# The beginning of an attention and two expert layers: another order for the first row of maxima and for unit 1's loads and halves

## The chip, the cores and the metric

The kernel runs on one core of a Trainium2 chip. The metric is the device time of one execution in microseconds (us); a core has the engines PE (matrix multiply), DVE (vector), ACT (activation functions), POOL (general purpose) and SP (which here only issues transfers). Each engine executes its own instructions strictly in the order in which the program lists them; ACT, POOL and SP also issue transfers (DMA) between the main memory and the core.

## The reference, cut to what matters

Attention with a decay bias over 4 batches of 8 heads, 576 positions and 64 columns, then a layer of 8 experts that are chosen token by token, then a layer with a convolution gate. Only the attention's start is touched:

```
scores = scale * q @ k.T                       # 576 x 576 per head
cum    = cumsum(max(s, 0))                     # decay, one number per position
scores = where(causal, -1e9, scores + min(-(cum_i - cum_j), 0))
attn   = exp(scores - max(scores)); attn /= sum(attn) + 1e-9
out    = attn @ v
x      = expert layer(out);  y = gated layer(x)
```

## The kernel before

**Units and steps.** The attention works in 8 units of 4 heads (two units to a batch). A unit has 14 steps; a step computes one 128x512 tile of scores on PE (`scores`, L481 with a mask L484), one step later ACT takes the exponentials (`weights`, L520, or the pair L525 and L526), two steps later DVE subtracts to get the low half (`rest`, L537), four steps later PE multiplies by v (`values`, L553). Tiles of scores are in three buffers `z`, so the scores of a step can only be written when the exps and the subtraction of three steps before are done.

**Halves.** Each f32 number of q and k is held as two f16 halves. For a unit: load q and k (`load`, L165), scale to the high half on ACT (`split_hi`, L258), subtract to get the low half on DVE or on POOL (`split_lo`, L264 or L266 and L267), turn both by transposing transfers that SP issues (`turn`, L276), copy one part on DVE (`copy`, L284). In unit 0 PE does the turning (`turned`, L297; evacuated by ACT at L300 and by DVE at L302). The last 64 positions of all heads ("tails") go the same way: `load_tail` L193, `tail_hi` L288, `tail_lo` L292, `turn_tail`, `copy_tail` L326, rows of the decay by `extra_tail` L322.

**Maxima.** Before a unit's scores can be used, a row of maxima must stand in its k tile: `stage_a` computes scores once without the low halves in pieces (PE L381 into two buffers `za`), DVE takes the maximum of each piece (L384, L412), PE turns them (`max_turn`, L449), ACT copies them (`max_out`, L454), and a small transfer of two issues puts them in place (`max_row`, L461; the tail's is L464). The scores of the unit (L481) read that row. For unit 0 this is done in halves: pieces 0 to 5 for heads 0 and 1 (`pa`, then `mt0a`, `mo0a`, `mr0a`), pieces 6 to 11 for heads 2 and 3 (`pb`, `pc`, `pd`, then `mtb`, `mob`, `mrb`), pieces 12 to 14 for the tails (`pt`, then `mtt`, `mot`, `mrt`). Unit 0's scores begin with heads 0 and 1 (seven steps, 0 to 6); step 7 is the first that needs the second half's row. For unit 0 ACT issues these transfers, for the others SP.

**What sets the order.** A table `PAR` of numbers. `start` gives each task of the beginning a time: negative ones run in that order ahead of step 0, others in the step of their whole part, ahead of that step's scores on PE. For units 1 to 7 the numbers are steps counted from the unit's first step (14 times its number): `load` and `loadq`, `at` (split k, split q, the two transposes, the extra rows), `cp` (the copies), `sv` (halves of v), `pa` and `pn` (first step and spread of the maxima's pieces), `mx` (turning the maxima). Because engines run in order, the number decides what an instruction waits behind on each engine.

Of the kernel before, what the change touches and what calls it, by code (L numbers as in the profile page):

```python
# [42 lines left out]
class Keep:  # L43
# [6 lines left out]
PAR = {'u1': {'sv': -6, 'pa': -7, 'pn': 5, 'mx': -3},  # L50
 'u2': {'at': (-24, -23, -21, -20.9, -20), 'cp': (-16, -15), 'lv': -11, 'sv': -2, 'pa': -14, 'pn': 8, 'mx': -6},
 'u3': {'load': -37, 'loadq': 1, 'at': (-33, -30, -28, -27, -26.9), 'cp': (-21, -20), 'sv': -1, 'pa': -20, 'pn': 14, 'mx': -6},
 'u': {'load': -51,
# [22 lines left out]
           'thk': -29,  # L76
           'hk1': -28,
           'hq1': -27,
           'wm': -26,
           'pa': -25,  # L80
           'mt0a': -24,
           'mo0a': -23,
           'mr0a': -22,
           'thq': -21,
           'lk1': -20,
           'tlk': -19,
           'tlq': -18,
           'lq1': -17,
           'xt': -16,
           'lk2': -15,  # L90
           'lq2': -14,
           'T1k': -13,
           'T1q': -12,
           'x1': -11,
           'ttk': 0.6,
           'ttq': 1.0,
           'pb': 1.1,
           'ct': 2.0,
           'pt': 2.1,
           'sv0': 2.4,  # L100
           'c2': 2.5,
           'mtt': 3.0,
           'mot': 3.1,
           'mrt': 3.2,
           'pc': 3.3,
           'pd': 4.0,
           'mtb': 5.0,
           'mob': 5.1,
           'mrb': 5.2,
           'z': 6.0,  # L110
# [9 lines left out]
def attention(tc, ctx, q, k, v, s, xd, rt, hook):  # L120
# [7 lines left out]
    nc = tc.nc  # L128
# [131 lines left out]
    def split_lo(u, n):  # L260
        i = AT[n]
        a, h = U[u, n].rearrange("p h c (t d) -> p (h c t) d", t=2), U[u, "h"][:, i]
        if u < 1 or (u, n) == (1, "k"):
            V.scalar_tensor_tensor(h[:, :, i], in0=a, scalar=scale[n], in1=h[:, :, 1 - i], op0=ALU.mult, op1=ALU.subtract)  # L264
        else:
            G.tensor_scalar(a, a, scale[n], 0.0, op0=ALU.mult, op1=ALU.add)  # L266
            G.tensor_tensor(h[:, :, i], a, h[:, :, 1 - i], op=ALU.subtract)  # L267
# [188 lines left out]
    def max_row(u, hs=slice(0, 4), tails=True):  # L456
        n, Q = 0, nc.sync if u else nc.scalar
        if hs:
            n = 4 * (hs.stop - hs.start)
            for e in range(2):  # L460
                Q.dma_start(U[u, 1][70:71, e, 1, 256 * hs.start:256 * hs.stop].rearrange("o (x c) -> o x c", c=128), U[u, "mr", key(hs)][n // 2 * e:n // 2 * e + n // 2])  # L461
        if tails:
            c = 256 * (u % 2)
            Q.dma_start(T1[70:71, u // 2, 1, c:c + 256].rearrange("o (r c) -> o r c", r=2), U[u, "mr", key(hs)][n:n + 2])  # L464
# [185 lines left out]
    copy(0, "q")  # L650
    for n in ("k", "q"):
        load(1, n)
    load_tail("q")
    todo, pieces, copies = {}, {}, {5: [(1, "k")], 6: [(1, "q")]}

    def plan(t, f):
        todo.setdefault(math.floor(t), []).append((t, len(todo), f))
# [13 lines left out]
    def second_a(r):  # L671
# [11 lines left out]
        mtb=lambda: max_turn(0, second, False), mob=lambda: max_out(0, second, False), mrb=lambda: max_row(0, second, False),  # L683
        xt=extra_tail, ct=copy_tail, lk2=lambda: load(2, "k"), lq2=lambda: load(2, "q"),
        T1k=lambda: [turn(1, e, slice(0, 1)) for e in range(2)], T1q=lambda: [turn(1, e, slice(1, 2)) for e in range(2)], x1=lambda: extra(1),
# [13 lines left out]
    for u in range(1, NU):  # L699
        t0 = u * PER  # L700
        c = PAR.get(f"u{u}", {}) if u < 4 else PAR.get("u", {})
        if u > 1:
            if u > 2:
                plan(t0 + c["load"], lambda u=u: load(u, "k"))
                plan(t0 + c["load"] + c["loadq"], lambda u=u: load(u, "q"))
# [872 lines left out]
```

## Time and profile before

| | us |
|---|---|
| time, median of 3 runs (lowest to highest) | 710.66 (709.4 to 717.71) |
| time of the profiled execution | 709.87 |
| its span in the profile | 708.2 |
| PE busy in the span | 644.5 (91%) |
| DVE busy | 451.3 (64%) |
| ACT busy | 390.4 (55%) |
| POOL busy | 253.1 (36%) |

An engine's busy time says how much of the span it worked; it does not say what the others waited for. The views below do: a timeline lists an engine's instructions in order with the wait ahead of them, and the table of windows gives the busy time, the granted PE clock and the transfers of a stretch.

### The profile page before, as it was taken

What the parts mean: (1) busy time and instruction counts of PE and PEld (TensorE: products, weight loads), DVE (VectorE), ACT (ScalarE), POOL (GpSimd) and SP (SyncE); (2) the same over time, 40 slices, a digit from 0 to 9 for tenths busy, and PEclk for the clock granted to TensorE, in tenths of its full rate; (3) what the DMA queues carried; (4) which work ended last, traced back from release to release, by engine and by line L of the source; (5) the groups of instructions that cost most, each with busy time, mean ns of one, the idle gap of its engine ahead of it and who ended that gap; (6) DMA issues with size and microseconds to landing.
All of it is one profiled execution on the core that took longest, in us unless ns stands there. A gap on an engine that the chain in (4) does not pass through costs nothing. (4 is left out here: it accounts for less than half of the span.)

```text
span 708.2 us, 15490 instructions
## 1 busy us (share of the span) xinstructions
PE 644.5 (91%) x5177; PEld 403.8 (57%) x5177; DVE 451.3 (64%) x858; ACT 390.4 (55%) x660; POOL 253.1 (36%) x358
## 2 busy tenths in 40 slices
PE   5478999899999656999999999999889999999997
PEld 2346778688888533444444444444367766665443
DVE  7565788978876699563886867763039975546000
ACT  5451867778688656552845564532049964645111
POOL 7635976646332049932254453433100000000000
PEclk9765799989999869999999999999999999999999
DMA  5964686755547436899999998944195000000111
GB/s 144 185 145 73 113 162 128 175 113 97 159 135 264 128 100 198 241 304 293 258 277 266 289 234 245 220 129 82 50 169 101 1 16 19 28 31 30 45 46 59
DMA packets 168828, 101.82 MB, mean 144 GB/s; under 512 B 119712, under 2 KB 147016, under 8 KB 168732
## 3 DMA queue, kind: packets, MB, share of 16 engines
q1 hardware_dynamic: 164712, 88.65, 51.7%
q0 software_dynamic: 3984, 11.99, 5.6%
q8 instruction: 47, 0.77, 0.5%
q14 instruction: 49, 0.40, 0.2%
q10 hardware_dynamic: 36, 0.00, 0.0%
HBM read 62.18 MB, written 15.31 MB: 109 GB/s over the span
## 5 line engine op out<-in xcount | busy, mean ns | idle before, releaser
L1188 PE MATMUL hp<-r,xt 128*128 x504 | 113.9, 383 | 6.6 <-ACT xt L1219 6.6
L1188 PE MATMUL yp<-r,ht 128*128 x504 | 112.2, 379 | 1.7 <-PEq L1295 1.1
L1386 PE MATMUL hp<-yt,wi 128*128 128x288 f16 x768 | 95.6, 286 | 2.6 <-DMA yt<-yd 2.6
L1434 PE MATMUL o<-wo,g 128*128 128x512 f16 x432 | 94.5, 379 | 0.0
L1386 PEld LDWEIGHTS <-wi 128*128 128x128 f16 x768 | 75.1, 98 | 23.5 <-DMA yt<-yd 2.8
L1188 PEld LDWEIGHTS <-xt 128*128 128x128 f16 x504 | 49.7, 99 | 67.1 <-ACT xt L1219 7.7
L1188 PEld LDWEIGHTS <-ht 128*128 128x128 f16 x504 | 48.5, 98 | 57.4 <-issue 1.8
L1144 DVE SCALAR_TENSOR_TENSOR r<-st,r 128x512 f32 (+3 forms) x80 | 70.8, 952 | 6.7 <-ACT r L1133 5.0
L1434 PEld LDWEIGHTS <-g 128*128 128x128 f16 x432 | 42.3, 98 | 49.5
L384 DVE TENSOR_REDUCE mx<-za 128x1 f32<-128x384 f32 (+4 forms) x97 | 57.4, 603 | 18.7 <-PE za L381 18.2
L1133 ACT ACTIVATE r<-st 128x512 f32 (+3 forms) x84 | 57.1, 763 | 22.1 <-SPq L1181 12.9
L525 ACT ACTIVATE phi<-z,lnes 128x512 f16<-128x512 f32 (+1 forms) x80 | 50.6, 633 | 33.0 <-PE z L484 31.5
L1249 POOL DMA_INDIRECT yd<-ys,idx x21 | 23.9, 1136 | 122.6 <-DVEq L1172 77.7
L481 PE MATMUL z<-k 71*128 71x256 f16 (+2 forms) x320 | 54.8, 298 | 12.1 <-DMA k<-mr 8.7
L537 DVE TENSOR_TENSOR plo<-z,phi 128x512 f16<-128x512 f32 (+1 forms) x80 | 48.2, 603 | 11.0 <-ACT z L526 10.5
L1403 DVE SCALAR_TENSOR_TENSOR c<-hb,cw,c 128x576 f32<-128x576 f32 x32 | 26.1, 816 | 35.5 <-ACT c L1397 35.5
L526 ACT ACTIVATE z<-z,lnes 128x512 f32<-128x512 f32 (+1 forms) x80 | 48.5, 607 | 0.0
L553 PE MATMUL o<-v,p 128*128 128x65 f32 x256 | 47.1, 297 | 0.0
L1437 ACT ACTIVATE s<-o 128x512 f32<-128x512 f32 x18 | 10.7, 597 | 63.2 <-PE o L1434 63.2
L1247 ACT ACTIVATE ys<-yp,pp 128x512 f16<-128x512 f32 x21 | 14.3, 683 | 53.6 <-PE yp L1188 35.7
L553 PE MATMUL o<-vv,phi 128*128 128x65 f16 (+1 forms) x512 | 43.2, 206 | 0.0
L553 PEld LDWEIGHTS <-phi 128*128 128x128 f16 x544 | 42.8, 111 | 0.0
(285 smaller groups left out, 1201.5 us busy)
## 6 DMA issues: line engine op xcount, KB each, us to landing
st<-in_moe_w_dram SPq DMA_DIRECT2D x8, 2048.0 KB
st<-in_moe_w_dram SPq DMA_DIRECT2D x24, 512.0 KB
out_dram<-s SPq DMA_DIRECT2D x18, 256.0 KB
st<-in_k_dram SPq DMA_DIRECT2D x16, 256.0 KB
st<-in_q_dram SPq DMA_DIRECT2D x16, 256.0 KB
xd<-xh SPq DMA_DIRECT2D x16, 256.0 KB
k<-in_moe_w_dram SPq DMA_DIRECT2D x8, 512.0 KB
s<-in_moe_w_in_dram SPq DMA_DIRECT2D x16, 256.0 KB
```

What stands on the lines that cost most here:

```text
L384: return lambda: V.tensor_reduce(out, z.rearrange("p (e c) -> p e c", e=m), axis=AX.X, op=ALU.max)
L481: PE.matmul(out, lhsT=ks[i], rhs=qs[i], start=first and not i, stop=False, skip_group_check=True)
L525: A.activation(hi[:, 0:n], z[:, 0:n], AF.Exp, bias=lnes, scale=1.0 / SC)
L526: A.activation(p[:, 0:n], z[:, 0:n], AF.Exp, bias=lnes, scale=1.0 / SC)
L537: (V if md == "a" else G).tensor_tensor(lo[:, 0:n], p[:, 0:n], hi[:, 0:n], op=ALU.subtract)
L553: PE.matmul(out, lhsT=w, rhs=x, start=first, stop=last, skip_group_check=True)
L1133: i = self.nc.scalar.activation(hi, src, AF.Copy, scale=self.scale[w])
L1144: i = nc.vector.scalar_tensor_tensor(lo, in0=src, scalar=sc, in1=hi, op0=ALU.mult, op1=ALU.subtract)
L1188: i = self.nc.tensor.matmul(out, lhsT=lhsT, rhs=self.rings[w][:, c, k, bass.ds(s, 1), f], **kw)
L1386: PE.matmul(st[x][:, n, 0:HN], lhsT=wi[:, c, k, m], rhs=t[:, n, a + k], start=k + a + c == 0, stop=k == 3 and a == 4)
L1403: V.scalar_tensor_tensor(c, in0=h[:, 1:S + 1], scalar=cw[:, m, 1:2], in1=c, op0=ALU.mult, op1=ALU.add)
L1434: PE.matmul(o, lhsT=g[:, a, k, 128 * i:128 * i + 128], rhs=wo[:, c, k], start=j == 0, stop=j == 23)
```

## The change

In the beginning's table the tasks are put in another order, and four lines follow from it.

- The first half's row of maxima (`mr0a`) is issued by SP, and not by ACT. On SP it stands between unit 1's load of k and its load of q (`ldq1` is a new task; ahead of it the tails of q are loaded, which came behind unit 1's loads).
- ACT copies the first maxima (`mo0a`) straight after the tail's high half of k; unit 1's high halves (`hk1`, `hq1`) stood ahead of it. `hk1` now follows the tail's high half of q, `hq1` the first exp.
- Unit 1's low half of q is made by DVE (was POOL) in step 2, and its transposes, its extra rows and the loads of unit 2 are issued in step 2 (were ahead of step 0).
- The pieces `pc` and `pd` come at 2.2 and 3.3 (were 3.3 and 4.0), the second row of maxima at 4.4 to 4.6 (was 5.0 to 5.2), the halves of v for unit 0 (`sv0`) at 5.4 (was 2.4).
- Units 2 and 3 have some numbers a step or two later; no load of units 3 and 4 is issued ahead of step 7.

The rows of the table `start` that the text speaks of, and the rest of the diff:

```
- 'u2': {'at': (-24, -23, -21, -20.9, -20), 'cp': (-16, -15), 'lv': -11, 'sv': -2, 'pa': -14, 'pn': 8, 'mx': -6},
+ 'u2': {'at': (-22, -21, -19, -18.9, -18), 'cp': (-14, -13), 'lv': -11, 'sv': -2, 'pa': -12, 'pn': 7, 'mx': -6},
...
-           'sv0': 2.4,
...
+           'sv0': 5.4,
...
-        if u < 1 or (u, n) == (1, "k"):
+        if u < 2:
...
-        n, Q = 0, nc.sync if u else nc.scalar
+        n, Q = 0, nc.sync if u or hs == first else nc.scalar
...
-    for n in ("k", "q"):
-        load(1, n)
     load_tail("q")
+    load(1, "k")
...
-                plan(t0 + c["load"], lambda u=u: load(u, "k"))
+                plan(max(t0 + c["load"], 7), lambda u=u: load(u, "k"))
```

The changed program's lines are one higher (L165 is L166 there). SP, ahead of and in step 0, before: the 12 small rows of the decay (L318), unit 1's k and q (L165, two transfers each), the tails of q (L193), the tails' decay rows (L322), unit 2's k and q, the four transposes of unit 1 (L276).

```order
L318 DMA k_138<-cp 1x4x256 x12
L165 DMA st_112<-in_k_dram 128x4x128 x2
L165 DMA st_112<-in_q_dram 128x4x128 x2
L193 DMA k_143<-in_q_dram 32x8x128 x4
L322 DMA t_141<-ext 3x4x512 x2
L165 DMA st_111<-in_k_dram 128x4x128 x2
L165 DMA st_112<-in_q_dram 128x4x128 x2
L276 DMA_TRANSPOSE k_391<-st_111 128x16x64 x4
L280 DMA k_139<-ex 3x2x1024 x2
L165 DMA st_112<-in_k_dram 128x4x128 x2
L165 DMA st_111<-in_k_dram 128x4x128 x2
```

The same place of SP after the change:

```order
L319 DMA k_138<-cp 1x4x256 x12
L194 DMA k_143<-in_q_dram 32x8x128 x4
L166 DMA st_112<-in_k_dram 128x4x128 x2
L462 DMA k_138<-mr 1x4x128 x2
L166 DMA st_112<-in_q_dram 128x4x128 x2
L323 DMA t_141<-ext 3x4x512 x2
L277 DMA_TRANSPOSE k_384<-st_111 128x16x64 x4
L281 DMA k_139<-ex 3x2x1024 x2
L166 DMA st_111<-in_k_dram 128x4x128 x2
L166 DMA st_112<-in_q_dram 128x4x128 x2
```

The first row of maxima (L462) is new on SP, in front of unit 1's q; unit 2's loads moved from ahead of unit 1's transposes to behind its extra rows.

ACT, from the tail's high half of k (L288) on, before; L258 is unit 1's high halves, L454 and L461 the first maxima, L300 the tails' evacuation, L520 the exp of step 0, L341 the halves of v:

```order
L288 ACTIVATE k_144<-k_143 128x16x64
L258 ACTIVATE st_111<-st_112 128x16x64 x2
L454 ACTIVATE mr<-mt 8x128
L461 DMA k_138<-mr 1x4x128 x2
L288 ACTIVATE k_144<-k_143 128x16x64
L300 ACTIVATE t_142<-o 128x4x128 x4
L520 ACTIVATE p_473<-z,lnes 128x512
L341 ACTIVATE vv<-nv 128x16x64
L341 ACTIVATE vvt<-nvt 128x2x64
L525 ACTIVATE phi<-z,lnes 128x512
L526 ACTIVATE z<-z,lnes 128x512
L454 ACTIVATE mr<-mt 2x128
```

After, the same stretch, and what follows it:

```order
L289 ACTIVATE k_144<-k_143 128x16x64
L455 ACTIVATE mr<-mt 8x128
L289 ACTIVATE k_144<-k_143 128x16x64
L259 ACTIVATE st_111<-st_112 128x16x64
L301 ACTIVATE t_142<-o 128x4x128 x4
L521 ACTIVATE p_462<-z,lnes 128x512
L259 ACTIVATE st_111<-st_112 128x16x64
L526 ACTIVATE phi<-z,lnes 128x512
L527 ACTIVATE z<-z,lnes 128x512
L455 ACTIVATE mr<-mt 2x128
L465 DMA t_141<-mr 1x2x128
L521 ACTIVATE p_539<-z,lnes 128x512
```

```order
L521 ACTIVATE p_539<-z,lnes 128x512
L455 ACTIVATE mr<-mt 8x128
L462 DMA k_138<-mr 1x4x128 x2
L526 ACTIVATE phi<-z,lnes 128x512
L527 ACTIVATE z<-z,lnes 128x512
L342 ACTIVATE vv<-nv 128x16x64
L342 ACTIVATE vvt<-nvt 128x2x64
L526 ACTIVATE phi<-z,lnes 128x512
L527 ACTIVATE z<-z,lnes 128x512
```

The copy of the first maxima (now L455) moved up past three instructions and its transfer left ACT; one of unit 1's two high halves (L259) now stands between the exps of steps 0 and 1, and the halves of v (L342) between those of steps 3 and 4.

DVE, from unit 1's low half of k (L264) to the first maximum of the tails (L384, 128x2, behind the copies L326), before and after:

```order
L264 SCALAR_TENSOR_TENSOR st_111<-st_112,st_111 128x16x64
L292 SCALAR_TENSOR_TENSOR k_144<-k_143,k_144 128x16x64 x2
L302 CAST t_142<-z 128x4x128 x4
L384 TENSOR_REDUCE mx<-za 128x2 x2
L326 COPY t_141<-t_142 64x4x512 x2
L384 TENSOR_REDUCE mx<-za 128x2
L412 ISA za,mx<-za,zero,mx 128x512
```

```order
L293 SCALAR_TENSOR_TENSOR k_144<-k_143,k_144 128x16x64 x2
L265 SCALAR_TENSOR_TENSOR st_111<-st_112,st_111 128x16x64
L303 CAST t_142<-z 128x4x128 x4
L385 TENSOR_REDUCE mx<-za 128x2 x2
L327 COPY t_141<-t_142 64x4x512 x2
L265 SCALAR_TENSOR_TENSOR st_111<-st_112,st_111 128x16x64
L385 TENSOR_REDUCE mx<-za 128x2
L413 ISA za,mx<-za,zero,mx 128x512
```

Unit 1's low half of k (L265 after) moved behind the two low halves of the tails (L293), and the low half of q came to DVE, between the tails' copies (L327) and the tails' maxima.

## Rows read from the trace of the kernel before

**Rows 1.** The page's first line.

```profile
span 708.2 us, 15490 instructions
```

**Rows 2.** Waits of PE over the span: engine, line, releaser: us, times, longest.

```profile
PE z L481 <- DMA k<-mr: 8.7, 2, 5.7
```

**Rows 3.** Timeline of PE: start, length, engine, line, operation [idle before <-releaser].

```profile
18.88 0.39 PE L449 MATMUL mt<-ident,mx 128*8 128x128 f32 x2 [0.78 <-DVE mx L384]
...
28.20 1.04 PE L481 MATMUL z<-k 71*128 71x512 f16 x2 [5.74 <-DMA k<-mr]
...
32.77 0.87 PE L481 MATMUL z<-k 71*128 71x128 f16 x6
...
36.33 0.69 PE L481 MATMUL z<-k 71*128 71x512 f16 x2
...
39.84 1.06 PE L481 MATMUL z<-k 71*128 71x128 f16 x6
...
47.98 1.03 PE L481 MATMUL z<-k 71*128 71x512 f16 x2 [2.99 <-DMA k<-mr]
```

**Rows 4.** Timeline of ACT (ACTq: its queue issuing a transfer).

```profile
17.82 1.06 ACT L258 ACTIVATE st<-st 128x1024 f16<-128x1024 f32 x1 [3.36 <-DMA st<-in_k_dram]
20.56 1.06 ACT L258 ACTIVATE st<-st 128x1024 f16<-128x1024 f32 x1 [1.68 <-DMA st<-in_q_dram]
21.52 0.25 ACT L454 ACTIVATE mr<-mt 8x128 f16<-8x128 f32 x1
21.80 1.79 ACTq L461 DMA_DIRECT2D k<-mr  x2
...
31.73 1.06 ACT L341 ACTIVATE vv<-nv 128x1024 f16<-128x1024 f32 x1
32.67 0.31 ACT L341 ACTIVATE vvt<-nvt 128x128 f16<-128x128 f32 x1
...
44.54 1.23 ACTq L461 DMA_DIRECT2D k<-mr  x2
...
46.40 0.65 ACT L526 ACTIVATE z<-z,lnes 128x512 f32<-128x512 f32 x1
```

**Rows 5.** Timeline of SP's queue.

```profile
13.85 0.99 SPq L165 DMA_DIRECT2D st<-in_k_dram  x2
14.88 1.06 SPq L165 DMA_DIRECT2D st<-in_q_dram  x2
15.98 2.17 SPq L193 DMA_DIRECT2D k<-in_q_dram  x4
...
28.22 7.40 SPq L276 DMA_TRANSPOSE k<-st  x4
...
70.61 1.40 SPq L461 DMA_DIRECT2D k<-mr  x2
```

**Rows 6.** Timeline of DVE.

```profile
18.91 1.23 DVE L264 SCALAR_TENSOR_TENSOR st<-st,st 128x1024 f16<-128x1024 f32 x1
...
33.73 1.40 DVE L326 COPY t<-t 64x2048 f16<-64x2048 f16 x2
```

**Rows 7.** Windows: from:to length, PE busy, granted PE clock, share and GB/s of the transfers.

```profile
13.85:21.00 7.15, 3.70 (x25) 1.00 0.89 213
23.00:28.20 5.20, 0.00 (x0) 0.51 0.98 204
```

**Rows 8.** Transfers by kind: queue, count, size of each, median us to landing where known.

```profile
st<-in_k_dram SPq DMA_DIRECT2D x16, 256.0 KB
...
k<-in_q_dram SPq DMA_DIRECT2D x4, 128.0 KB
...
nv<-in_v_dram POOLq DMA_DIRECT2D x8, 64.0 KB, 6.1
```

**Rows 9.** Windows, all engines: busy PE, PEld, DVE, ACT, POOL (instructions), clock, transfers.

```profile
48.00:85.00 37.00, 34.13 (x289) 27.49 (x290) 23.16 (x48) 17.14 (x33) 23.00 (x36) 0.60 0.61 109
85.00:120.00 35.00, 32.47 (x463) 26.85 (x460) 31.18 (x72) 26.31 (x50) 28.38 (x58) 1.00 0.69 142
```

## What I expect of the change

> **What bounds the beginning now.** The page's chain of waits is followed back only into the last third of the span, where PE works without a pause; it says nothing of the beginning. So I read the waits of PE first: over the whole span its largest wait is for the row of maxima, 8.7 us in two waits [rows 2]. PE's timeline shows where they are: 5.74 us ahead of the scores of step 0, which start at 28.20, and 2.99 us ahead of those of step 7 (the first of heads 2 and 3), which start at 47.98 [rows 3]. The order behind them is fixed on every engine, so what these two starts gain is what the program can gain, unless something else comes last in their place. The span is 708.2 us, the time of that execution 709.87 [rows 1].
>
> The reader should follow the first row back. PE has turned the maxima at 18.88 + 0.39 = 19.27 [rows 3], but ACT copies them only at 21.52: ahead of that copy stand unit 1's two high halves, and both waited for their loads, 3.36 and 1.68 us [rows 4]. Then ACT issues the two transfers, 21.80 + 1.79 = 23.59, and the row is there at 28.20, 4.61 us after the last issue. For the second row the issue ends at 44.54 + 1.23 = 45.77 and the scores start at 47.98, only 2.21 us later [rows 3, 4]. So 2.4 us of the first row's way is not the transfer itself. What differs is the traffic: in 23.00:28.20 the transfers run at 204 GB/s with a share of 0.98 [rows 7], because SP has been loading without a break.
>
> **The first row, step by step.** Without the two high halves ahead of it, ACT copies the maxima at 19.27 and is done after 0.25, at 19.52 [rows 4]. SP is free by then: the tails of q go out from 13.85 for 2.17 us and unit 1's k for 0.99, until 17.01 [rows 5]. Two such issues take SP 1.40 us [rows 5], so the last is out at 20.92. Its landing is not in the trace; 2.21 and 4.61 us are the two ends. Ahead of it are then the tails of q (4 of 128 KB), unit 1's k (2 of 256 KB) and POOL's loads of v (8 of 64 KB), 1.5 MB (1.57 million bytes) [rows 8]; at the 213 GB/s of 13.85:21.00 [rows 7] 7.15 us move 1.52 million. The queue is all but empty when the row is issued, as it was for the second row, and unit 1's q comes behind it. I take 2.21: step 0 starts at 23.1, **5.1 us** earlier; with 4.61 it would be 25.5, 2.7 earlier.
>
> **Step 1.** Its scores come 32.77 - 28.20 = 4.57 us after step 0's [rows 3], behind 16 transposes of the tails and two pieces of maxima. These need DVE and ACT to have emptied the tiles of the first 16. On DVE unit 1's low half of k now stands ahead of that. Unit 1's k is out at 17.01 and lands 2.98 us (14.84 to 17.82) to 4.62 us (15.94 to 20.56) later [rows 4, 5], by 21.6; 1.06 for the high half [rows 4] and 1.23 for the low half [rows 6] make 23.9, when step 0's scores (1.04 us) are still running. So the gain is kept: step 1 at 27.7.
>
> **What is given back: step 2.** Here DVE gets work that POOL had, unit 1's low half of q, between the copies of the tails and the tails' maxima: 1.23 us by the row of k's half [rows 6]. Behind it wait the tails' maxima, behind those the two buffers of pieces, and on PE the scores of step 2. The copies started 33.73 - 32.77 = 0.96 after step 1's scores and took 1.40 [rows 3, 6]: now 28.7 to 30.1, with the half until 31.3. From the end of the copies to step 2's scores it was 36.33 - 35.13 = 1.2 [rows 3, 6]. In addition `pc`, two pieces, now stands ahead of step 2 and not of step 3. Two such pieces stood between step 2's and step 3's scores, which are 3.51 us apart [rows 3]; I put half of that to them, 1.7 (an estimate, with bounds of 0 and 3.5). Step 2 then starts at 31.3 + 1.2 + 1.7 = 34.2, only **2.1 us** earlier than 36.33. Step 3 has `pd` ahead of it, at the same price: 37.7 against 39.84.
>
> **The second row, and step 7.** From `pd` to the end of the second row's copy go two reductions, a turn and a copy; by the first row's pieces (0.39 and 0.25 [rows 3, 4], and for a reduction of 512 columns an estimated 0.6, half of the 1.23 that DVE takes for 1024 [rows 6]) that ends at 39.2, the issue (1.23) at 40.4, and the row is there at 42.6 to 45.0. It was 47.98. But ACT has more to do now. Its issue, the exps of step 3 (twice 0.65), the halves of v (1.06 + 0.31) and the exps of step 4 stand in one line [rows 4]; before, the halves of v ran at 31.73, while ACT waited for PE anyway. 40.4 + 1.3 + 1.4 + 1.3 = 44.4, and with step 4's subtraction on DVE (0.6 by the same estimate) its buffer is free for step 7 at 45.0. So step 7 starts at 45.0, set by ACT and no longer by the row: **3.0 us** earlier. The bounds are 5.4 earlier, if only the row binds (42.6), and 0.6, if the first landing takes the longer 4.61 (45.0 + 2.4 = 47.4).
>
> **What costs nothing.** POOL loses the q half: it is hidden, since no wait of PE's there is for POOL, and SP's transposes of q only follow DVE now. SP issues them from 31.3 on at 7.40/4 = 1.85 us each [rows 5], until 35.0, where they ended at 35.62 before; the copies that read them stay in steps 5 and 6. Unit 2's later numbers shift work by two steps inside steps where PE is busy 34.13 of 37.00 us [rows 9]; if that cover were gone it would be one copy or half, about 1.2 us. From step 7 on the instructions are the same, and I carry the 3.0 us to the end.
>
> **Sum.** 709.87 - 3.0 = 706.9 us. The median of the three runs, 710.66, is 0.8 above the profiled time, and the runs spread over 8 us; 2% of it, 14.2 us, is about what a measurement of this kernel can tell from no change.
>
> **Rival 1, the clock stays high.** The granted clock is 1.00 until 23 and 0.51 over 23.00:28.20, in which PE does nothing [rows 7]; step 0's scores then run at the lower of the two levels, 1.2 GHz, and over 48.00:85.00 the mean is 0.60, against 1.00 in 85.00:120.00 [rows 9]. PE fell idle at 28.20 - 5.74 = 22.46 and would now wait only until 23.1. If the clock is kept, and kept again at step 7, PE no longer sets the pace of 48:85; DVE would, with 23.16 us of work, at the share it reaches at full clock, 31.18 of 35.00: 23.16 / 0.89 = 26 us for 37, 11 us less. With the 3.0 that is **696 us**. Against it: at the full clock PE soon waits for DVE and ACT in steps 2 to 7 as worked out above, and each such wait is what took the clock away before. The Trainium skill (TensorE: Matmul & The Clock Gate, Part 1) says that the lowered clock is the default and that activity releases it; by that rule this rival's time would hold, and the trace agrees in that the clock of 23.00:28.20 fell where PE stood idle.
>
> **Rival 2, the row lands no sooner.** It still shares its engines with the loads of v. Then steps 0 to 7 keep only what the earlier issue gives, 0.6 us at step 7: **709.3 us**. For it speaks the full share of the transfers until 21.00 [rows 7].
>
> **Rival 3, slower: SP stands still and unit 2 comes late.** SP now waits for the maxima, and everything behind them waits too: unit 2's k goes out only behind unit 1's transposes (35.0) and two small issues (1.40), until 37.4. It lands at 40.4 to 42.0 by the two landings above. ACT scales it behind the exps of step 4, at 44.4. If it lands after that, the exps of step 5 and the scores behind them wait too. The margin is 2.4 us; the time passes the old one when ACT starts later than 47.3, a landing of 9.9 us, twice the longest of the rows. With 12 us, twice the 6.1 that POOL's loads of v took [rows 8], ACT starts at 49.4, 2.1 later than allowed: **712 us**. The Trainium skill (DMA: Bandwidth & Descriptors, Anatomy of one DMA) says that a transfer's wait for a semaphore happens on the issuing sequencer before dispatch; by that rule a waiting row holds back every load behind it on SP. No row shown here tells of it by itself.
>
> **Chances.** Forecast 0.53 (its own range 704.5 to 709.3), rival 1 0.17, rival 2 0.20, rival 3 0.10. The range of 697 to 712 leaves out most of rival 1's half beyond its price and a little of rival 3. Faster by over 2% (below 696.4) is half of rival 1, 0.08; slower by over 2% I give 0.02, since no priced mechanism reaches 14 us; the rest, 0.90, is within.
>
> **What would show it.** Right: step 0's scores near 23 with a wait of under 1.5 us, step 2's near 34, ACT without a pause from 40 to 44, step 7's near 45. Rival 1 shows as a clock near 1.00 in the 25 us behind step 7; rival 2 as step 0 at 25 or later with the wait still for the row; rival 3 as ACT waiting for unit 2's load ahead of step 5's exps. The forecast is wrong if the difference at step 7 is not the one at the end: then a later stage took or gave it.

## The result, and the profile after the change

The changed kernel takes 716.77 us (median of 20 executions, 712.76 to 723.02) against 713.25 us before (20 executions, 709.22 to 717.71): a ratio of 1.0055, interval 1.0032 to 1.0078. It is slower by half a percent, about 4 us, where 3.0 us less was forecast. Part of the distance to the forecast time is the base: the profiled execution of before (709.87 us) was one of its quick ones, 3.4 us below the median of 20. Two profiles of the same kernel here differ in span by up to 7 us (712.2 and 719.0 for the changed kernel), so one profile is read for places and ratios are read for sizes.

The beginning went as the prediction says up to step 3. PE's wait for the row of maxima [rows 2] is down to one of 1.6 us; the page's first line and that wait after the change:

```profile
span 712.2 us, 15489 instructions
```

```profile
PE z L482 <- DMA k<-mr: 1.6, 1, 1.6
```

PE's timeline (start, length, engine, line, operation, then the wait ahead of it and what ended it; lines after the change are one higher, L482 for L481), to be held against [rows 3]:

```profile
23.50 1.03 PE L482 MATMUL z<-k 71*128 71x512 f16 x2 [1.59 <-DMA k<-mr]
...
27.95 0.62 PE L482 MATMUL z<-k 71*128 71x128 f16 x6
...
34.30 1.06 PE L482 MATMUL z<-k 71*128 71x512 f16 x2
...
37.80 0.74 PE L482 MATMUL z<-k 71*128 71x128 f16 x6
...
45.21 0.37 PE L482 MATMUL z<-t 71*128 71x128 f16 x2 [4.77 <-DVE plo L538]
46.65 1.01 PE L482 MATMUL z<-k 71*128 71x512 f16 x2 [0.96 <-DMA nv<-in_v_dram]
```

Step 0 starts at 23.50 (was 28.20), steps 1, 2 and 3 at 27.95, 34.30 and 37.80, step 7 at 46.65 (was 47.98). ACT's and SP's timelines give the row's way, as [rows 4, 5] did:

```profile
19.75 0.27 ACT L455 ACTIVATE mr<-mt 8x128 f16<-8x128 f32 x1 [4.80 <-PE mt L450]
...
39.60 1.24 ACTq L462 DMA_DIRECT2D k<-mr  x2
...
42.04 1.05 ACT L342 ACTIVATE vv<-nv 128x1024 f16<-128x1024 f32 x1
...
43.75 0.67 ACT L527 ACTIVATE z<-z,lnes 128x512 f32<-128x512 f32 x1
44.32 1.07 ACT L259 ACTIVATE h<-st 128x1024 f16<-128x1024 f32 x1
```

```profile
20.04 1.20 SPq L462 DMA_DIRECT2D k<-mr  x2
21.29 0.99 SPq L166 DMA_DIRECT2D st<-in_q_dram  x2
```

The last issue of the first row ends at 21.24, and the scores start 2.26 us later. On ACT the exps of step 4 end at 43.75 + 0.67 = 44.42, and unit 2's first half follows at once. What held step 7 up is on DVE, where the low halves of v (L346), and then one of unit 1's copies (L285), stand ahead of the subtractions (L538) that set the buffers of scores free:

```profile
38.66 0.68 DVE L538 TENSOR_TENSOR plo<-z,phi 128x512 f16<-128x512 f32 x1
43.12 1.23 DVE L346 SCALAR_TENSOR_TENSOR vv<-nv,vv 128x1024 f16<-128x1024 f32 x1 [3.79 <-ACT vv L342]
44.27 0.29 DVE L346 SCALAR_TENSOR_TENSOR vvt<-nvt,vvt 128x128 f16<-128x128 f32 x1
44.47 0.68 DVE L538 TENSOR_TENSOR plo<-z,phi 128x512 f16<-128x512 f32 x1
45.18 0.69 DVE L285 COPY k<-k 64x2048 f16<-64x2048 f16 x1
45.90 0.69 DVE L538 TENSOR_TENSOR plo<-z,phi 128x512 f16<-128x512 f32 x1
```

DVE stands idle for 3.79 us waiting for ACT's high half of v, while step 3's exps on ACT end at 41.47 + 0.65 = 42.12. Its subtraction comes only at 44.47, and step 4's, behind the copy, at 45.90. PE starts step 6 at 45.21, and step 7 at 46.65, 0.06 us after step 4's subtraction ends. The view puts this last wait down to a load of v, which step 7 does not read; in after_again, the same kernel once more, it names DVE for the same wait:

```profile
46.90 1.01 PE L482 MATMUL z<-k 71*128 71x512 f16 x2 [0.96 <-DVE plo L538]
```

**Where the lead goes.** The copies of the finished maxima of unit 1 and of unit 2 on ACT mark the next 50 us; first before, then after:

```profile
70.32 0.27 ACT L454 ACTIVATE mr<-mt 18x128 f16<-18x128 f32 x1 [8.71 <-PE mt L449]
...
93.76 0.27 ACT L454 ACTIVATE mr<-mt 18x128 f16<-18x128 f32 x1 [1.53 <-PE mt L449]
```

```profile
68.63 0.27 ACT L455 ACTIVATE mr<-mt 18x128 f16<-18x128 f32 x1 [8.38 <-PE mt L450]
...
93.75 0.27 ACT L455 ACTIVATE mr<-mt 18x128 f16<-18x128 f32 x1 [5.22 <-PE mt L450]
```

At unit 1's row the changed kernel is 1.69 us ahead, at unit 2's row 0.01. Three windows up to there (from:to, length, then busy time of PE, PEld, DVE, ACT and POOL with instructions, granted PE clock, share and GB/s of the transfers), before and after:

```profile
84.00:88.00 4.00, 3.34 (x50) 2.64 (x48) 2.83 (x8) 3.60 (x7) 3.77 (x8) 1.00 0.36 81
88.00:92.00 4.00, 3.45 (x42) 2.55 (x42) 3.76 (x10) 1.57 (x5) 3.33 (x18) 1.00 0.89 201
92.00:96.00 4.00, 3.71 (x42) 2.80 (x40) 3.96 (x9) 2.47 (x6) 3.36 (x19) 1.00 0.69 184
```

```profile
84.00:88.00 4.00, 2.87 (x33) 2.14 (x33) 3.91 (x6) 3.43 (x9) 3.92 (x5) 1.00 0.76 172
88.00:92.00 4.00, 2.04 (x20) 1.36 (x20) 3.94 (x11) 0.53 (x1) 3.35 (x20) 1.00 0.61 142
92.00:96.00 4.00, 3.62 (x25) 2.55 (x25) 2.12 (x6) 2.25 (x5) 3.50 (x14) 0.58 1.18 219
```

After the change DVE is full for 8 us (7.85 of 8.00) and PE works 4.91 of them, 1.88 less than before; then the granted clock falls to 0.58. PE's timeline names the releaser, DVE's maxima of unit 2 (L385 and, for the tails, L413). Below it stand PE's waits for them between the two copies on ACT (total, times, longest), first before, then after:

```profile
84.78 0.38 PE L382 MATMUL za<-k 70*128 70x512 f16 x1 [0.80 <-DVE mx L385]
...
90.93 0.62 PE L382 MATMUL za<-k,t 70*64 70x512 f16 x4 [1.19 <-DVE mx L385]
92.38 0.38 PE L382 MATMUL za<-k 70*128 70x128 f16 x4 [0.83 <-DVE mx L413]
```

```profile
PE za L381 <- DVE mx L384: 1.1, 2, 0.9
```

```profile
PE za L382 <- DVE mx L385: 2.7, 5, 1.2
PE za L382 <- DVE mx L413: 0.8, 1, 0.8
```

So 3.5 us of waits stand where 1.1 stood. These two profiles show where the lead goes, but not the loss itself: the first product behind the attention comes at 235.98 after the change and at 236.72 before, so the changed kernel is still 0.74 us ahead there. What makes its span 4.0 us longer (712.2 against 708.2) lies behind the attention, in a stretch that scatters by more than that (below). That the loss comes from unit 2's maxima rests on the ratios of the runs that follow.

### The profile page after: what moved, and what is told of

Read it like the earlier page. It is cut to its first block, busy times and chain, and to the rows that moved or that the text cites. A ratio compares the mean times of both kernels' runs of the same rounds, so it can differ in the third digit from the quotient of the medians.

```text
span 712.2 us, 15489 instructions
## 1 busy us (share of the span) xinstructions
PE 644.6 (91%) x5177; PEld 403.9 (57%) x5177; DVE 451.5 (63%) x859; ACT 390.5 (55%) x660; POOL 248.1 (35%) x356
## 5 line engine op out<-in xcount | busy, mean ns | idle before, releaser
L1386 PE MATMUL hp<-yt,wi 128*128 128x288 f16 x768 | 97.1, 289 | 4.2 <-DMA yt<-yd 4.2
L385 DVE TENSOR_REDUCE mx<-za 128x1 f32<-128x384 f32 (+4 forms) x97 | 57.2, 602 | 19.2 <-PE za L382 18.6
L482 PE MATMUL z<-k 71*128 71x256 f16 (+2 forms) x320 | 54.0, 295 | 6.0 <-DVE plo L538 2.4
L538 DVE TENSOR_TENSOR plo<-z,phi 128x512 f16<-128x512 f32 (+1 forms) x80 | 48.2, 603 | 10.9 <-ACT z L527 10.3
```

Of the source, the lines that this page charges most:

```text
L385: return lambda: V.tensor_reduce(out, z.rearrange("p (e c) -> p e c", e=m), axis=AX.X, op=ALU.max)
L482: PE.matmul(out, lhsT=ks[i], rhs=qs[i], start=first and not i, stop=False, skip_group_check=True)
L538: (V if md == "a" else G).tensor_tensor(lo[:, 0:n], p[:, 0:n], hi[:, 0:n], op=ALU.subtract)
L1386: PE.matmul(st[x][:, n, 0:HN], lhsT=wi[:, c, k, m], rhs=t[:, n, a + k], start=k + a + c == 0, stop=k == 3 and a == 4)
```

## Experiments

All ratios are to the kernel before, run beside it on the same chip, with the 95% interval. The ratios all lie within 1% of 1, so it is the intervals that tell kernels apart. The table gives, of each kernel's one profile, the start of step 7, ACT's copies of unit 1's and unit 2's rows, and the first product behind the attention (L927, in some L929 or L931), in us; the clock is the median over the executions of the mean granted clock (not listed for before).

| kernel | step 7 | unit 1's row | unit 2's row | behind attention | clock | ratio |
|---|---|---|---|---|---|---|
| before | 47.98 | 70.32 | 93.76 | 236.72 | | 1 |
| before_again | 49.39 | 72.54 | 96.64 | 240.04 | 0.942 | 0.9971 [0.9942, 1.0000] |
| after | 46.65 | 68.63 | 93.75 | 235.98 | 0.938 | 1.0055 [1.0032, 1.0078] |
| after_again | 46.90 | 69.12 | 98.49 | 243.63 | 0.937 | 1.0029 [1.0001, 1.0056] |
| unit2_maxima_in_8_steps | 45.55 | 68.43 | 92.62 | 232.72 | 0.944 | 0.9980 [0.9951, 1.0009] |
| unit2_copies_early | 46.80 | 69.72 | 96.09 | 238.32 | 0.937 | 1.0036 [1.0004, 1.0068] |
| unit2_maxima_in_7_steps_from_14 | 45.55 | 68.46 | 93.19 | 232.86 | 0.944 | 0.9990 [0.9962, 1.0017] |
| unit2_shorter_reductions | 47.71 | 69.89 | 97.55 | 240.31 | 0.940 | 0.9999 [0.9974, 1.0024] |
| before_with_unit2_maxima_in_6_steps | 47.49 | 70.82 | 98.52 | 241.08 | 0.936 | 1.0036 [1.0005, 1.0068] |
| v_halves_early_in_7_steps | 45.77 | 67.59 | 96.76 | 243.34 | 0.933 | 1.0022 [0.9994, 1.0050] |
| v_halves_early_and_8_steps | 44.16 | 66.07 | 89.90 | 229.44 | 0.941 | 0.9939 [0.9912, 0.9965] |
| v_halves_early_and_8_steps_again | 43.94 | 65.82 | 90.50 | 232.87 | 0.944 | 0.9945 [0.9915, 0.9976] |
| v_halves_early_and_9_steps | 44.23 | 66.14 | 91.28 | 236.66 | 0.939 | 0.9988 [0.9967, 1.0010] |
| q_half_on_pool_and_8_steps | 49.02 | 70.84 | 94.42 | 237.16 | 0.941 | 0.9999 [0.9970, 1.0028] |
| unit3_two_steps_later | 45.29 | 67.17 | 91.92 | 234.64 | 0.939 | 1.0029 [0.9997, 1.0062] |
| eight_steps_unit3_later | 44.15 | 66.90 | 90.11 | 231.01 | 0.942 | 0.9944 [0.9906, 0.9982] |
| nine_steps_unit3_later | 42.77 | 65.56 | 89.20 | 230.41 | 0.946 | 0.9905 [0.9868, 0.9942] |
| after_filled | 47.08 | 69.99 | 96.79 | 237.89 | 0.941 | 1.0041 [1.0009, 1.0072] |
| nine_steps_filled | 43.88 | 66.64 | 93.03 | 235.76 | 0.944 | 0.9997 [0.9966, 1.0028] |
| nine_steps_unit3_later_filled | 44.01 | 66.81 | 93.28 | 234.96 | 0.944 | 0.9985 [0.9952, 1.0018] |

The six profiles whose attention ends before 233 us belong to ratios of 0.9905 to 0.9990, the others to 0.9971 and more. This is a tendency of single profiles: two of the changed kernel end their attention at 235.98 and 243.63. The time from there to the end of the span is 471.5 us (before) to 479.6 us (unit3_two_steps_later) and shows no tie to an edit or to the ratio; it is taken as scatter.

A steadier mark is PE's wait for DVE's maxima between the two rows. It adds up to 3.1 to 3.5 us in after, after_again, unit2_copies_early, v_halves_early_in_7_steps and v_halves_early_and_9_steps (ratios 0.9988 to 1.0055). It is 1.0 or 1.1 us in before, before_again and the six profiles in which unit 2's maxima stand in steps 14 to 20 or 14 to 21 (ratios 0.9939 to 1).

### The two kernels again, and unit 2's numbers of before

before_again and after_again are the two kernels unchanged.

> The kernel before, unchanged, for a second trace and as the measure of scatter: ratio 1.000 within 0.3%. Theory 'maxima of unit 2': its end of attention (the scores' last tile) falls where it did, near 232 us, and unit 2's row of maxima near 94. Theory 'experts' stage': its time in the expert stage differs from the first trace by several us although nothing changed.

> The changed kernel, unchanged, for a second trace: ratio 1.005 within 0.3%. Theory 'maxima of unit 2' expects again some 3.7 us of lead at the scores ahead of unit 2's row of maxima (near 88 us) and none behind it (near 94). Theory 'experts' stage' expects that the lead or loss at the end of attention is under 1 us again and that 3 to 5 us are lost behind it.

```
- 'u2': {... 'cp': (-14, -13), ... 'pa': -12, 'pn': 7, 'mx': -6},
+ 'u2': {... 'cp': (-16, -15), ... 'pa': -14, 'pn': 8, 'mx': -6},
```

> The changed kernel with unit 2's copies and maxima at the steps of before (copies in steps 12 and 13, pieces from step 14 over 8 steps). Theory 'maxima of unit 2': DVE has more steps for the pieces, the lead of 3.7 us ahead of unit 2's row is kept, so 3 us less than the changed kernel: ratio 1.001 or below. Theory 'the start' (the loss lies in SP's wait and DVE's added half): 1.005, no change. Theory 'experts' stage': attention ends up to 3 us earlier, the total does not follow.

Before against itself comes to 0.9971, so a difference of 0.3% in one series is at the edge of what these runs tell apart. The changed kernel is slower in the second measurement too (1.0029). With unit 2's maxima in steps 14 to 21 again it falls to 0.998; the order of the beginning is unchanged by that (that step 7 comes at 45.55 and not at 46.65 is scatter: eight profiles with this order up to step 7 have 45.29 to 47.71). In its profile PE is busy for 6.32 of 8 us at 84 to 92, and the clock stays up:

```profile
84.00:92.00 8.00, 6.32 (x84) 4.73 (x82) 7.71 (x17) 4.24 (x9) 6.89 (x23) 1.00 0.64 144
92.00:100.00 8.00, 7.90 (x122) 7.19 (x120) 6.14 (x17) 6.00 (x12) 6.45 (x19) 1.00 0.85 144
```

So unit 2's later numbers cost 0.5 to 0.75% (3.5 to 5.3 us of 713), and the order of the beginning without them gains about 1.4 us by this run (0.2%, with an interval that includes none, and 0.9971 for before itself beside it): a gain of the beginning alone is not shown here.

### Which of unit 2's numbers it is

unit2_copies_early is the changed kernel with only `cp` put back; unit2_maxima_in_7_steps_from_14 has `cp` and `pa` put back, and keeps the 7 steps.

```
unit2_copies_early:               'cp': (-16, -15), 'pa': -12, 'pn': 7
unit2_maxima_in_7_steps_from_14:  'cp': (-16, -15), 'pa': -14, 'pn': 7
```

> The changed kernel, with only the two copies of unit 2's turned halves on DVE two steps earlier, in steps 12 and 13 as before the change; its maxima stay in the 7 steps from step 16. It tells the two halves of unit2_maxima_in_8_steps apart. Theory A1 (the maxima, squeezed into 7 steps, are what DVE can't keep up with): unit 2's row of maxima comes 25 us or more behind unit 1's, the ratio to the kernel before stays at 1.001 to 1.005. Theory A2 (the copies, 1.26 us each, stand ahead of the maxima of unit 2 and of unit 1's last work and cause the wait): interval 24.2 us as in unit2_maxima_in_8_steps, ratio 0.998.

> The changed kernel with unit 2's copies in steps 12 and 13 and its maxima from step 14 as before the change, but still spread over 7 steps (14 to 20) and not 8. Theory A1 (seven steps are too few): interval between unit 1's and unit 2's rows of maxima 25 us or more, ratio 1.001 to 1.005. Theory A3 (what counts is that the maxima begin two steps later and so end close to unit 2's first step, not how many steps they take): ratio 0.997 to 0.999, interval as in unit2_maxima_in_8_steps or shorter.

1.0036 and 0.9990: the copies don't matter (A2 falls), and seven steps are not too few (A1 falls). What matters is that the maxima begin two steps later, A3 (their intervals overlap by a little: 1.0004 and 1.0017). PE's waits for DVE's maxima between the two rows, the first from 16, the second from 14:

```profile
PE za L382 <- DVE mx L385: 2.3, 4, 1.2
PE za L382 <- DVE mx L413: 0.8, 1, 0.8
```

```profile
PE za L382 <- DVE mx L385: 1.0, 1, 1.0
```

PE's busy time alone does not tell the two apart: in the 8 us ahead of unit 2's row it is 5.69 us in the first and 5.41 us in the second, but with a clock of 0.93 and of 1.00.

The exact converse, the kernel before with only unit 2's `cp`, `pa` and `pn` of the change (only_unit2_maxima_in_7_steps), has no time: in that order its instructions wait for one another in a circle, a deadlock. In its place stands another squeeze in the kernel before, `'pa': -14, 'pn': 8` to `'pa': -13, 'pn': 6`: one step later and not two, and in 6 steps.

> The kernel before, with one edit: unit 2's maxima begin one step later (step 15 of the attention's steps, not 14) and are spread over 6 steps and not 8. The beginning up to step 14 is that of the kernel before. Theory A (the squeeze costs by itself): between the copies of unit 1's and unit 2's rows of maxima lie 25 to 27 us instead of 23.4 to 24.1, PE waits for DVE's maxima in these steps, and the time is 1.5 to 4 us longer: ratio 1.002 to 1.006. Rival (the loss of the changed kernel comes from its beginning or from the experts' stage and not from unit 2's maxima): interval 23.4 to 24.1 and a ratio of 1.000.

1.0036 with 27.7 us between the two rows (before: 23.4): a squeeze of unit 2's maxima alone, with the old beginning, costs about what the whole change costs. Its profile shows another part of the price than the changed kernel's does: PE waits only 1.3 us for DVE's maxima there, but the clock is 0.50 from 72 to 88 us, where it is back at 81 in before and at 84 in before_again. So the wait that theory A named is not what this profile shows.

### Is it DVE's pace?

In the changed kernel the reductions of unit 2 were cut to part of their columns:

```
+            if u == 2:
+                n = z.shape[2]
+                z = z[:, :, {128: 0, 256: 128, 384: 128, 512: 256, 64: 0}[n]:n]
```

> The changed kernel with unit 2's maxima in the same 7 steps from 16, but DVE's reductions of unit 2 read 256 of 512 and 256 of 384 columns (part of each maximum is left out), about 2 us less of DVE's work in these steps; PE's pieces are unchanged. Theory A (DVE's pace in these steps is what PE waits for): PE's waits for DVE's maxima there shrink by about 2 us, the interval falls from 25.1 to some 23.5, and the ratio comes to 0.998 to 1.001. Rival (PE's pieces are in the way by themselves, or the loss lies behind the attention): PE's work is the same, the ratio stays at 1.003 to 1.0055.

The ratio is 0.9999, as the theory had it, with PE's pieces unchanged (its interval, up to 1.0024, is clear of the first measurement of the changed kernel, from 1.0032, and overlaps that of after_again, from 1.0001). DVE's 14 reductions, 12 of unit 2 and two of unit 3, take 6.2 us in 70 to 100, where the changed kernel's 14 in 70 to 96 take 8.1 (groups by line: line, engine, operation, count, busy us and mean ns, idle time before):

```profile
L389 DVE TENSOR_REDUCE mx<-za 128x1 f32<-128x256 f32 (+4 forms) x14 | 6.2, 466 | 4.9 <-PE za L382 4.8
```

```profile
L385 DVE TENSOR_REDUCE mx<-za 128x1 f32<-128x384 f32 (+4 forms) x14 | 8.1, 616 | 3.0 <-PE za L382 3.0
```

The interval between the rows, expected at 23.5, was 27.7 in its one profile: that execution had a span of 717.1 us and a lower clock in this stretch (0.79 and 0.85 in 84 to 100), and says little of the median, 713.96. PE's waits for DVE's maxima between the rows are 2.3 us in it, against 3.1 to 3.5.

### The halves of v

`sv0` goes back from 5.4 to 2.4, once with unit 2's maxima in 8 steps and once with those of the change.

```
-           'sv0': 5.4,
+           'sv0': 2.4,
```

> Unit 2's maxima are spread over 8 steps from step 14 as before the change, and the halves of v for unit 0 go back from step 5 to step 2. Theory A (the lead of the beginning counts as long as unit 2's maxima do not take it back; the subtraction of step 3 on DVE stands behind the low half of v, 1.23 + 0.29 us, and PE waits for it ahead of step 7): step 7's scores start at 44.0 to 44.5 instead of 45.6 to 46.9, and the time lies 1.2 to 1.5 us below that of unit2_maxima_in_8_steps, at a ratio of about 0.996. Theory B (a lead at step 7 is lost behind it anyway, whatever unit 2's maxima do): step 7 earlier, but the ratio stays at 0.998 to 1.003. Theory C (the halves of v only move the wait: DVE now stands still for them in step 2, where it already has unit 1's low half of q): steps 2 and 3 come 1.2 to 1.5 us later and step 7 not earlier than 45.5, ratio 0.998.

> The changed kernel with the halves of v back in step 2, unit 2's maxima still squeezed into 7 steps from step 16. Theory A: step 7's scores start up to 1.5 us earlier than in the changed kernel (46.65), but unit 2's row of maxima comes at 93.7 as before, since DVE paces the 7 steps; the time is that of the changed kernel, a ratio of 1.003 to 1.006. Theory B': the halves of v are the whole of the loss: step 7 at 44 to 45 and a ratio of 0.998 or less, the row of maxima of unit 2 at 91 to 92.

> The same kernel as v_halves_early_and_8_steps, beside the others of this call. If its gain is the kernel's own and not that of one chip's runs, the ratio is 0.991 to 0.9965, the interval of its first measurement; otherwise it lies nearer to the 0.998 of unit2_maxima_in_8_steps.

With 8 steps it is 0.9939 and, on another chip, 0.9945; step 7 starts at 44.16, inside theory A's 44.0 to 44.5, and the gain on unit2_maxima_in_8_steps, 0.4%, is twice what it expected (the two intervals overlap, 0.9951 and 0.9965). That the halves set step 7 is clear of the scatter: from step 0 to step 7 it is 22.48 to 23.56 us in the eight profiles with `sv0` at 5.4 and the half of q on DVE, and 19.94 to 21.20 in the eight with 2.4. DVE makes the half at 34.99, in a gap, and step 3's subtraction waits for ACT's exp and for nothing else:

```profile
34.99 1.23 DVE L346 SCALAR_TENSOR_TENSOR vv<-nv,vv 128x1024 f16<-128x1024 f32 x1 [0.28 <-issue]
...
41.98 0.69 DVE L538 TENSOR_TENSOR plo<-z,phi 128x512 f16<-128x512 f32 x1 [3.02 <-ACT z L527]
```

Theory C falls: step 2 is at 33.91, where it was 33.89 without the edit, and step 7 is early (step 3 is 0.92 us later, 37.42 against 36.50). With the maxima in 7 steps from 16 the same edit leaves 1.0022, a little under theory A's 1.003 to 1.006: unit 2's row comes at 96.76, and the 0.9 to 1.1 us that step 7 gained on the changed kernel are gone. So a lead at step 7 does reach the end, but only when unit 2's maxima let it through.

### Unit 1's low half of q on POOL again

```
-        if u < 2:
+        if u < 1 or (u, n) == (1, "k"):
```

> unit2_maxima_in_8_steps with unit 1's low half of q made by POOL again and not by DVE. Theory A (the prediction's term of 1.23 us on DVE ahead of the tails' maxima sets step 2): step 2's scores start about 1.2 us earlier than 34.3, at 33.1, step 3 with it; step 7 not earlier than 45, since the low half of v still stands ahead of step 3's subtraction; ratio 0.997 to 0.999. Rival (the pieces of maxima, not the half, set step 2): step 2 at 34.3 as in the changed kernel, or later if the transposes of q that wait for POOL hold up unit 2's load; ratio 0.998 or more.

Theory A missed, and the rival had a later step 2 and a ratio of 0.998 or more, but for another reason than the one found. Step 2 comes at 36.86, 2.97 us later than in unit2_maxima_in_8_steps, and the ratio is 0.9999. Of these 2.97 us 1.36 are there at step 0 already (24.29 against 22.93), ahead of the edit. From step 0 to step 2 it is 12.57 us against 10.96, 1.61 more, where the other profiles of the new beginning have 10.08 to 10.97. PE waits 3.15 us for DVE's copies of the tails (L327). One of the two takes 2491 ns, where both take 688 otherwise; first here, then in v_halves_early_and_8_steps (minimum, median and maximum in ns):

```profile
L327 DVE COPY t<-t x2: 800/1646/2491, 29.8 to 30.6; 64x2048 f16<-64x2048 f16 x2
```

```profile
L327 DVE COPY t<-t x2: 686/688/689, 28.5 to 29.2; 64x2048 f16<-64x2048 f16 x2
```

The slow one runs from 30.6 to 33.1, and POOL's subtraction for the half of q lies across it:

```profile
30.15 2.44 POOL L268 TENSOR_TENSOR st<-st,st 128x1024 f16<-128x1024 f32 x1
```

Before the change POOL's half of q was done by 29.56 and the copies began at 33.73 [rows 6]; with the earlier beginning they meet. Giving the half to DVE is therefore no loss of 1.23 us at step 2: on POOL it would cost 1.61 us more.

### What the late maxima run into

In steps 20 and 21 of the changed kernel DVE also copies unit 3's turned halves, and unit 3's maxima begin in step 22. v_halves_early_and_9_steps stretches unit 2's maxima to step 22 (`'pa': -14, 'pn': 9`); the others move unit 3's work:

```
- 'u3': {... 'cp': (-22, -21), ... 'pa': -20, 'pn': 14, 'mx': -6},
+ 'u3': {... 'cp': (-19, -18), ... 'pa': -18, 'pn': 12, 'mx': -6},
```

> v_halves_early_and_8_steps with unit 2's maxima thinner still, over 9 steps (14 to 22). Theory A (the fewer pieces in one step, the less PE waits for DVE there): a ratio of 0.992 to 0.994, PE's waits for DVE's maxima between 70 and 98 us no longer than there. Rival (eight steps already suffice, since one or two pieces stand in a step either way): 0.994, the same. Against both: 0.996 or more if the row of maxima now comes too late for unit 2's first scores.

> The changed kernel with unit 3's copies on DVE in steps 23 and 24 (were 20 and 21) and unit 3's maxima over 12 steps from 24 (were 14 from 22); unit 2's maxima stay in the 7 steps from 16. Theory A4 (in steps 20 to 22 DVE has unit 2's last maxima, unit 3's copies and unit 3's first maxima, and PE waits for it): the ratio falls from 1.003 to 1.0055 to 0.998 to 1.000, and PE's waits for DVE between 82 and 94 us shrink by 1.5 to 2.5 us. Theory A5 (unit 2's row is merely too near to unit 2's first scores): 1.003 to 1.0055, as the changed kernel.

> v_halves_early_and_9_steps (ratio 0.9988), whose unit 2 maxima end in step 22, with unit 3's copies and maxima from steps 23 and 24 as above. Theory A4: the collision is gone, the ratio comes back to that of 8 steps, 0.993 to 0.995. Theory A5: 0.998 to 1.000, unchanged.

> v_halves_early_and_8_steps with unit 3's copies and maxima two steps later as above. There unit 2's maxima end in step 21, beside one or two of unit 3's copies. Theory A4: 0.991 to 0.994, up to 1.4 us below v_halves_early_and_8_steps. Theory A5: the same as v_halves_early_and_8_steps. Against both: 0.996 or more, if unit 3's maxima in 12 steps are now too dense.

Thinner is not better: 9 steps give 0.9988 where 8 give 0.9939 and 0.9945, so both theories written ahead of it fall. With unit 3's work out of the way the 9 steps come to 0.9905, the fastest kernel here (707.73 us, of 8 executions): the way of A4, and below its 0.993 to 0.995. The two profiles, 9 steps as such and with unit 3 later:

```profile
84.00:92.00 8.00, 5.61 (x61) 3.81 (x59) 6.88 (x15) 2.12 (x6) 6.92 (x35) 0.88 0.81 189
92.00:100.00 8.00, 8.00 (x64) 7.07 (x63) 2.93 (x6) 2.98 (x6) 3.99 (x6) 0.50 0.77 112
```

```profile
84.00:92.00 8.00, 6.71 (x84) 5.07 (x83) 6.48 (x15) 4.22 (x10) 6.62 (x32) 1.00 0.81 189
92.00:100.00 8.00, 7.60 (x137) 7.01 (x136) 7.86 (x20) 6.50 (x13) 5.89 (x8) 1.00 0.77 110
```

The changed kernel itself does not come back with unit 3 later (1.0029), which is against A4 as it was written. PE's waits for DVE's maxima in 82 to 94 shrank by 1.2 us, from 3.5 to 2.3, less than the 1.5 to 2.5 that A4 expected. In that profile the clock is low in 84 to 92 (0.52), so PE is busy for 6.75 us there, and not for 4.91, with no more instructions than the changed kernel (51, and 53 there):

```profile
84.00:92.00 8.00, 6.75 (x51) 3.98 (x51) 5.87 (x15) 2.69 (x7) 7.02 (x34) 0.52 0.78 190
```

With 8 steps, where unit 2's maxima end ahead of unit 3's, moving unit 3 changes nothing (0.9944), as A5 had it.

### Waits or clock?

Ahead of each of the last eight pieces of unit 2 PE multiplies twice into an idle tile; the kernels are the changed one, the one with 9 steps, and the fastest.

```
+            if u == 2 and i >= 6:
+                busy(mps.tile([128, 512], F32, name="mt"), 2)
```

> The changed kernel, with two needless 128x512 multiplications on PE (0.21 us each at the full clock) ahead of each of unit 2's last eight pieces of maxima, 3.4 us of work in steps 19 to 22, where PE waits 3.7 us for DVE. Theory B1 (the loss is the low clock behind these waits): the clock stays at 1.00 in 84 to 108 us, the execution's mean clock rises from 0.938 to 0.942 or more, and the ratio falls from 1.003 to 1.0055 to 0.998 to 1.000. Theory B2 (the loss is the waiting alone): the waits turn into work, nothing gets earlier, ratio 1.003 to 1.006, or up to 1.008 where the filling delays what did not wait.

> v_halves_early_and_9_steps (ratio 0.9988, clock 0.50 in 92 to 100 us of its profile) with the same filling ahead of unit 2's last eight pieces. Theory B1: no second fall of the clock, ratio 0.992 to 0.995. Theory B2: 0.998 to 1.001.

> nine_steps_unit3_later (ratio 0.9905, clock 1.00 from 78 us on in its profile) with the same filling. Here the clock does not fall, so both theories expect no gain: 0.990 to 0.993; what it lies above 0.9905 prices the filling itself. It also repeats, but for the filling, the measurement of the fastest kernel.

The clock does what B1 says: in the profiles of the first two it stays at 1.00 from 84 to 100 us (the changed kernel filled):

```profile
84.00:92.00 8.00, 7.13 (x86) 5.18 (x84) 6.45 (x14) 5.08 (x10) 7.47 (x22) 1.00 0.63 142
92.00:100.00 8.00, 7.69 (x80) 5.05 (x79) 6.81 (x17) 3.68 (x8) 6.99 (x25) 1.00 0.78 144
```

The times do what B2 says: 1.0041 and 0.9997, no gain. The third kernel shows that the filling is not free, 0.9985 against 0.9905, though the 0.9905 rests on 8 executions. In all three unit 2's row comes 26.4 to 26.8 us behind unit 1's. If the filling costs the changed kernel as much as it costs the third, the clock gave as much back, but that is argued, not shown. The runs do not separate the two parts of the loss.

## Why the prediction was wrong

- **Step 0, right.** 23.50 against 23.1; the landing was 2.26 us behind the last issue, the value of 2.21 that was chosen between 2.21 and 4.61. The 0.4 us come from ACT's copy, at 19.75 instead of 19.27, since PE turned the maxima that much later. Rival 2 (the row lands no sooner) is out.
- **Steps 1 to 3, right.** 27.95, 34.30 and 37.80 against 27.7, 34.2 and 37.7. The term of 1.7 us for `pc` is 1.66 (32.64 to 34.30), that of 1.23 for the half of q 1.21. That the half on DVE "is given back" was a wrong reading all the same, since on POOL it costs 1.61 us more by step 2 (q_half_on_pool_and_8_steps).
- **Step 7, a term left out.** ACT's line ends where it was forecast (the exps of step 4 at 44.42 against 44.4), by some luck. The issue ends at 40.84 and not at 40.4: the terms of the prediction, 37.7 + two reductions of 0.6 + 0.39 + 0.25 + 1.23, add up to 40.8. And ACT's work behind it took 3.58 us where 4.0 were summed up. But the prediction counted the halves of v on ACT alone. Their low halves stand on DVE ahead of the subtractions of steps 3 and 4, 1.23 + 0.29 us and a wait for ACT, and a copy of 0.69 us stands between the two. Step 7 came at 46.65 against 45.0; with `sv0` at 2.4 it comes at 44.16, 1.39 us ahead of 45.55. Of the 3.0 us 1.33 were there at step 7.
- **"What costs nothing": unit 2's later numbers, the step that failed.** The cover named was PE's in 48 to 85 [rows 9]. The moved maxima end at 93, and six of unit 2's 14 reductions (four of L385, two of L413) lie behind 85.5, where the row for 85 to 120 has the clock at 1.00 and DVE busy 31.18 of 35.00 us. The fallback price of 1.2 us, one copy, was too small as well: the runs put it at 0.5 to 0.75%, 3.5 to 5.3 us. Several waits of PE for DVE add up there, 3.5 us where 1.1 were, and the clock falls behind them; how much of the price is the waits and how much the clock stays open.
- **"From step 7 on the instructions are the same, and I carry the 3.0 us to the end", failed with it.** They are not the same, since unit 2's and unit 3's numbers lie behind step 7 too. The lead is 1.69 us at unit 1's row and 0.01 at unit 2's. With unit 2's maxima at 14 and the halves of v early the lead comes through: 3.82 us at step 7 in v_halves_early_and_8_steps, and a ratio of 0.9939.
- **Rivals 1 and 3** did not happen. The clock is 0.54 in 23.00 to 28.20, though PE is busy in 4.70 of these 5.20 us. It had fallen to 0.50 by 21, behind waits of 0.78 and 0.75 us, so the long wait that rival 1 blamed was not needed for it. ACT scales unit 2's load at 44.32 without a wait. None of the three rivals has the mechanism that decided, and the range ended at 712.

## What to carry to other kernels

A lead won early is worth what the next tight stage lets through: before carrying it to the end, find the first stage behind it in which another engine is nearly full, and look at what the same change does there. Here two steps of delay for work on DVE, written as an adjustment, cost 0.5 to 0.75%, more than the new beginning as written gained (0.2%, within the scatter). When one engine's work is listed as hidden, list its second half on the other engines too (the halves of v have a part on ACT and one on DVE, and DVE's stood ahead of what PE waited for).

## What the runs showed of the hardware

**DVE's copy stands still while POOL subtracts.** A copy of 64x2048 f16 on DVE took 2491 ns instead of 688 when it began half a microsecond behind the start of POOL's subtraction of 128x1024 (2.44 us); it ended at 33.1, POOL's at 32.59. It is no single case: every one of the 20 profiles has such a copy of 1.6 us or more beside a subtraction on POOL. In the kernel before:

```profile
73.29 2.27 DVE L284 COPY k<-k 64x2048 f16<-64x2048 f16 x1
```

```profile
72.75 2.12 POOL L267 TENSOR_TENSOR st<-st,st 128x1024 f16<-128x1024 f32 x1
```

It ends at 75.56, 0.69 us behind POOL's 74.87, as if it had only then begun. The Trainium skill (SBUF — State Buffer, SBUF: two separate sides) says that VectorE and GpSimd share a pair of ports, and that it is an exclusive lock: of a GpSimd instruction and a VectorE instruction in a mode that uses both port pairs, the first to start keeps it for its whole instruction. The trace agrees in that the copies ended 0.5 and 0.69 us behind POOL's instruction; whether the copy runs in such a mode no view here shows. In the changed kernel one such copy stands in the tight stretch itself: L285's at 86.08 takes 1.43 us and ends 0.55 us behind POOL's subtraction, which ends at 86.96.

**The clock goes with much of the scatter.** The 20 executions of the changed kernel run from 712.76 to 723.02 us, and their time goes with their mean granted clock: correlation -0.75, 4.2 us less for each 0.01 more. In 16 of the 18 other series it is -0.22 to -0.84; in v_halves_early_and_9_steps it is 0.09, and in nine_steps_unit3_later, with 8 executions, 0.61. Which of the two leads the other, a correlation does not tell. In the profiles shown the clock falls to 0.50 to 0.58 behind stretches in which PE waits repeatedly (in the changed kernel behind 84 to 92 us, with six waits of 0.16 to 1.19 us). Not each such stretch does it: in unit2_maxima_in_7_steps_from_14 PE is idle for 2.38 of the 8 us from 84 to 92, and the clock stays at 1.00 up to 104. What decides it was not settled. The Trainium skill (TensorE: Matmul & The Clock Gate, HAM oscillation — how this bites in real kernels) describes a kernel in which waits for transfers between groups of matmuls bring the low clock back each time. The trace agrees in the place, a stretch of repeated waits, but these waits are for DVE and shorter, 1.19 us at most in the changed kernel. Filling them kept the clock at 1.00 in the profiles, and the time did not fall.
